# Two attention blocks on one core: the remainder of P by DMA in 30 steps at other places, wq in quarter loads, the first x in three parts, output written in place

## The chip, the cores and the metric

The kernel runs on one core of one Trainium2 chip. The metric is the device time of one execution in microseconds (us). Profiles show one execution; the engines are called PE (TensorE matmul), PEld (its weight loads), DVE (VectorE), ACT (ScalarE), POOL (GpSimd) and SP (SyncE, which here only issues DMAs).

## The reference, cut to what matters

Two independent problems A and B of the same shapes, each a query projection, attention of grouped queries over a cache, and an output projection; the outputs are joined on the last axis. All inputs are bf16.

```python
B, Sq, D = 16, 80, 576
Hq, Hkv, Sk, Dh = 32, 16, 512, 128
def _A_ref(x, k_cache, v_cache, wq, wo):
    rep = Hq // Hkv                       # 2 query heads share one K/V head
    q = transpose((x @ wq).reshape(B, Sq, Hq, Dh), 0, 2, 1, 3)
    k = jnp.repeat(k_cache, rep, axis=1)  # k_cache, v_cache: (B, Hkv, Sk, Dh)
    v = jnp.repeat(v_cache, rep, axis=1)
    scores = jnp.einsum("bhqd,bhkd->bhqk", q, k) * (Dh ** -0.5)
    p = softmax(scores, axis=-1)
    o = jnp.einsum("bhqk,bhkd->bhqd", p, v)
    return transpose(o, 0, 2, 1, 3).reshape(B, Sq, Hq * Dh) @ wo
# B is the same with its own inputs
return jnp.concatenate([a, b], axis=-1)
```

## The kernel before

The work is cut into 128 **units**. A unit is one batch row and four K/V heads, so eight query heads of 80 rows: 640 rows of scores against 512 keys. These are five blocks of 128 rows: block 0 is the **remainder** (the last 32 of the 160 rows of each of the four K/V heads, put together), blocks 1 to 4 are the first 128 rows of each head.

For each unit, in this order:

- SP loads K with a transposing DMA (L631, one for two units) into one of three pairs of slots, and V (L635) into one of six slots.
- PE makes the scores: the remainders of two units together (L665, `SR`, in tiles of 32 columns), the other blocks in one matmul each (L678, `S`).
- DVE takes the negated maximum (L687), ACT the exponential with the row sum (L691), DVE the reciprocal (L697), POOL multiplies P by it (L700; `poolr` is the stream of the remainder, `pool` that of the other blocks). Remainders of P have four slots, the other blocks twelve.
- PE transposes P in pieces of 64 by 128 (L733, `T`): 40 matmuls, of which eight are the remainder's. ACT or DVE copies the result to `pT` (L751, L752; the remainder's part L757, L758, twice per unit).
- In some units, `rtr`, the remainder is transposed by a DMA from SBUF to SBUF instead (L740, stream `RT`, issued by SP): then `T` has 32 matmuls and the two copies of the remainder fall away. Before, these are the 27 odd units from 71 to 123. The DMA waits for POOL's normalisation of the remainder; PV of the unit waits for the DMA, and so does the exp that next writes the slot of P that it reads.
- PE multiplies `pT` by V (L781, `PV`), and ACT or DVE copies the result to `oT` (L795).

The query projection of an octet of query heads (L542, `Q`, four matmuls of 128 rows of D and the last 64 rows by L555, which stands in `T` or, at the start, in `QT`) is spread over earlier units; ACT or DVE copies it, scaled, to `qT` (L568, L569). Its weights are loaded eight times (four times for each problem) into one of two slots: `ldwa` at L507 and two small `ldwt` at L511. Before, the first two of these loads come in four pieces of 256 columns, the other six in one piece of 1024 KB.

The first problem's x is loaded (L380) and transposed on PE (L401, L419; POOL copies the last 64 columns beside them, L388); eight matmuls on zeros and ones (L353, `warm`) go ahead of that. The identity that the transposes need is made by POOL (L340). x lies, as bf16, in the memory of `acc`, the float32 accumulator of the output.

The output projection (L827, `P`, eight matmuls of 288 columns per half step) is also spread; the first half of the heads is copied to `acc` (L839), the second half is added to it by DVE into one of two slots of `osb` (L856), and SP stores the slot (L862): 40 stores.

Nothing is scheduled while the kernel runs. Each operation is put into a stream, sorted there by a key, and a string of 5227 operations (`ORDER`) gives the order over all streams: a letter names the stream, an apostrophe the second choice of engine (ACT in place of DVE for the copies), digits the PSUM banks. Each engine runs its operations in this order, and SP's queue is one of these: a DMA that waits holds all that stand behind it. Semaphore waits follow from reads and writes (`finalize`).

The names of the change in the old code:

```python
rtr = RT0 <= U < RT1 and (RTM[U % 2] or U >= RT2)          # L717
S.add("sp", 5.0 * U - 0.4, em_rtr, reads=[R(("P", psls[0]), ("n", 5 * U))],
      writes=[R(("pR", pts, h), U) for h in range(2)], dsem="d_r%d" % pts, ...)
pieces = () if half else [(256 * i_, 256 * i_ + 256) for i_ in range(4)] if goct < W4 else ((0, 1024),)
```

Of the kernel before, what the change touches and what calls it, by code (L numbers as in the profile page):

```python
# [26 lines left out]
NOSB = 2  # L27
NWARM = 8
# [3 lines left out]
RT0 = 71  # L32
RT1 = 124
RTM = (0, 1)
RT2 = 999
LQ = 12
# [15 lines left out]
XLD = ((-100.0, -85.0), (-5.0, -4.9))  # L52
# [3 lines left out]
W4 = 2  # L56
# [214 lines left out]
def bass_concat_heads__gqa_block_cached__gqa_block_cached__near_ridge_kernel(  # L271
# [27 lines left out]
    with ExitStack() as es:  # L299
# [33 lines left out]
        def R(res, ver):  # L333
            return (res, ver)
# [606 lines left out]
```

## Time and profile before

| what | value |
|---|---|
| time, median of 3 runs (lowest, highest) | 720.46 us (718.11, 721.86) |
| the profiled execution, its own time | 720.92 us |
| its span, first to last instruction | 719.0 us |
| granted TensorE clock | 1.00 |
| PE / PEld busy | 712.0 / 508.8 us |
| DVE / ACT / POOL busy | 630.0 / 637.5 / 431.9 us |
| a transposing load of K for two units, issue to landing | 8.4 to 8.5 us |
| a load of V | 5.0 to 5.2 us |
| a remainder of P by DMA | 4.2 us |
| wq: 256 KB / 1024 KB at a time | 4.7 / 6.9 to 8.4 us |
| a store of the output | 3.8 us |

Busy is the time that an engine's records cover. Matmuls are pipelined, so a covered PE need not be at its peak; the starts of matmuls say more. A line such as `SPq L740` is an entry of SP's queue. In the timeline the columns are start, duration, engine, line, operation, tiles and count; brackets give the idle time before and what ended it. In the windows the columns are the window, its length, then for each engine its busy time and number of instructions.

### The profile page before, as it was taken

The page shows a single profiled execution, that of the slowest core. Times are in us where ns is not written, and L with a number is a line of the kernel's source. Part 1 is how long each engine was busy: PE and PEld are TensorE (multiplying, and loading weights), DVE is VectorE, ACT ScalarE, POOL GpSimd, SP SyncE. Part 2 cuts the span into 40 slices and gives each one's busy share as a digit, 9 for nine tenths or more (in the row PEclk, how much of TensorE's full clock was granted, in tenths as well). Part 3 has the DMA queues.
Part 4 walks back from the last instruction along what each step waited for, and adds up shares of the span by engine and source line. Part 5 has one row for each costly group of instructions (what it writes and reads, how often), then busy time and mean ns, then how long its engine had stood idle before and what let it go on. Part 6 is the DMA issues. An engine that isn't in the chain of part 4 may idle for free.

```text
span 719.0 us, 25863 instructions
## 1 busy us (share of the span) xinstructions
PE 712.0 (99%) x10604; PEld 508.8 (71%) x10604; DVE 630.0 (88%) x1419; ACT 637.5 (89%) x1830; POOL 431.9 (60%) x650
## 2 busy tenths in 40 slices
PE   9999999999999999999999999999999999999998
PEld 5576777777777777777777776767677777777777
DVE  3999998899978998899998899878898889998995
ACT  1999998899988998799988999888999898998994
POOL 0467657566655765755774566645676466665783
PEclk9999999999999999999999999999999999999999
DMA  9999999999799998999999999999999999999970
GB/s 238 275 217 240 273 252 250 286 232 244 175 268 241 220 241 194 258 223 240 255 216 248 226 201 206 228 246 239 220 229 204 279 196 261 225 247 221 211 195 18
DMA packets 388853, 164.23 MB, mean 228 GB/s; under 512 B 293248, under 2 KB 385664, under 8 KB 388736
## 3 DMA queue, kind: packets, MB, share of 16 engines
q1 hardware_dynamic: 388736, 162.59, 100.2%
q8 instruction: 84, 1.38, 0.8%
q14 instruction: 33, 0.27, 0.2%
HBM read 87.65 MB, written 2.95 MB: 126 GB/s over the span
## 4 chain that ended last, share of the span: by engine, by line
PE 93%; DMA 2%; DVE 2%; ACT 1%; SPq 0%; issue 0%; ACTq 0%; DVEq 0%
PE ps L827 22%; PE ps L781 20%; PE ps L542 18%; PE ps L678 15%; PE ps L733 10%; PE ps L665 5%; PE ps L555 4%; DVE negmax L687 2%; DMA pT<-p_sb 1%; DMA wq_sb<-in_A_wq_dram 1%; DMA out_dram<-osb 1%; ACT p_sb L691 0%; ACT qT L568 0%; DVE xT L406 0%; DVE qT L569 0%
## 5 line engine op out<-in xcount | busy, mean ns | idle before, releaser
L700 POOL TENSOR_SCALAR p_sb<-p_sb,rinv 128x512 bf16<-128x512 bf16 x640 | 430.1, 692 | 271.4 <-DVE rinv L697 270.8
L691 ACT ACTIVATE p_sb<-ps,negmax 128x512 bf16<-128x512 f32 x640 | 442.7, 713 | 27.3 <-DVE negmax L687 23.5
L687 DVE TENSOR_REDUCE negmax<-ps 128x1 f32<-128x512 f32 x640 | 419.2, 682 | 35.0 <-PE ps L678 30.3
L781 PE MATMUL ps<-pT,v_sb 128*128 128x160 bf16 x2048 | 191.2, 233 | 1.1 <-ACT p_sb L691 0.8
L781 PEld LDWEIGHTS ps<-pT,v_sb 128*128 128x128 bf16 x2048 | 152.8, 98 | 42.6 <-ACT p_sb L691 4.1
L827 PE MATMUL ps<-wo_sb,oT 128*128 128x288 bf16 x1280 | 181.1, 286 | 0.0
L678 PE MATMUL ps<-kT,qT 128*128 128x512 bf16 x512 | 178.0, 380 | 1.2 <-ACT p_sb L691 0.8
L542 PE MATMUL ps<-xT,wq_sb 128*128 128x320 bf16 x1024 | 174.4, 299 | 0.2 <-DMA wq_sb<-in_A_wq_dram 0.2
L827 PEld LDWEIGHTS ps<-wo_sb,oT 128*128 128x128 bf16 x1280 | 122.0, 98 | 42.5 <-ACT p_sb L691 0.8
L691 ACT ACTIVATION_READ_ACCUMULATOR p_sb<-ps,negmax 128x1 f32 x640 | 146.0, 228 | 0.0
L542 PEld LDWEIGHTS ps<-xT,wq_sb 128*128 128x128 bf16 x1024 | 95.4, 98 | 45.0 <-ACT p_sb L691 2.4
L751 ACT COPY pT<-ps 128x512 f32<-128x512 f32 x157 | 92.4, 602 | 13.3 <-PE ps L733 12.8
L733 PEld LDWEIGHTS ps<-ident,p_sb 64*128 64x128 bf16 x4904 | 88.2, 95 | 7.3 <-issue 1.3
L733 PE MATMUL ps<-ident,p_sb 64*128 64x64 bf16 x4904 | 92.4, 190 | 0.3 <-issue 0.2
L752 DVE COPY pT<-ps 128x1024 bf16<-128x1024 bf16 x99 | 67.3, 684 | 11.4 <-PE ps L733 10.0
L568 ACT ACTIVATE qT<-ps 128x320 bf16<-128x320 f32 x133 | 59.0, 458 | 19.3 <-PE ps L555 15.5
L569 DVE TENSOR_SCALAR qT<-ps 128x320 bf16<-128x320 f32 x123 | 58.2, 482 | 10.7 <-PE ps L555 6.1
L795 DVE CAST oT<-ps 128x320 bf16<-128x320 f32 x122 | 58.4, 482 | 7.7 <-PE ps L781 7.4
L678 PEld LDWEIGHTS ps<-kT,qT 128*128 128x128 bf16 x512 | 48.0, 97 | 24.1 <-ACT p_sb L691 4.1
L795 ACT CAST oT<-ps 128x320 bf16<-128x320 f32 x134 | 58.9, 451 | 5.2 <-PE ps L781 4.9
L697 DVE RECIPROCAL rinv<-rowsum 128x3 f32<-128x3 f32 (+1 forms) x256 | 38.4, 160 | 1.8 <-ACT p_sb L691 1.7
L665 PE MATMUL ps<-kT,qT 128*32 128x512 bf16 x512 | 39.2, 384 | 0.0
(31 smaller groups left out, 175.5 us busy)
## 6 DMA issues: line engine op xcount, KB each, us to landing
v_sb<-in_A_v_cache_dram SPq DMA_DIRECT2D x64, 512.0 KB, 5.0
v_sb<-in_B_v_cache_dram SPq DMA_DIRECT2D x64, 512.0 KB, 5.2
wo_sb<-in_A_wo_dram SPq DMA_DIRECT2D x8, 576.0 KB, 5.8
wo_sb<-in_B_wo_dram SPq DMA_DIRECT2D x8, 576.0 KB, 5.8
wq_sb<-in_B_wq_dram SPq DMA_DIRECT2D x4, 1024.0 KB, 6.9
out_dram<-osb SPq DMA_DIRECT2D x40, 72.0 KB, 3.8
wq_sb<-in_A_wq_dram SPq DMA_DIRECT2D x8, 256.0 KB, 4.7
wq_sb<-in_A_wq_dram SPq DMA_DIRECT2D x2, 1024.0 KB, 8.4
```

Source lines behind the costliest of these rows:

```text
L542: last = e.matmul(ps[:, vbq[h].phys, QO:QO + 320], lhsT=wq_sb[:, wsl, ck, hi * 128:(hi + 1) * 128], rhs=xT[:, half, ck, n0:n0 + 320], star ...
L665: last = e.matmul(ps[32 * g4:32 * g4 + 32, vb_.phys, :], lhsT=qT[:, qsl_, bl_, g4 * 160 + 128:g4 * 160 + 160], rhs=k_of(U_, g4), start=Tru ...
L678: return e.matmul(ps[:, vb.phys, :], lhsT=qT[:, qsl, bl, gl * 160:gl * 160 + 128], rhs=k_of(U, gl), start=True, stop=True)
L687: return e.tensor_reduce(negmax[:, si:si + 1], ps[:, vb.phys, :], axis=AX.X, op=AluOpType.max, negate=True)
L691: return e.activation(p_sb[:, psl, :], ps[:, vb.phys, :], AF.Exp, bias=negmax[:, si:si + 1], scale=1.0, accum_out=rowsum[:, ss, k:k + 1])
L700: return e.tensor_scalar(p_sb[:, psl, :], p_sb[:, psl, :], rinv[:, ss, k:k + 1], 1.0, op0=AluOpType.mult, op1=AluOpType.mult)
L733: last = e.matmul(dst, lhsT=p_sb[64 * h:64 * h + 64, psls[k_], j * 128:(j + 1) * 128], rhs=ident[64 * h:64 * h + 64, 64 * h:64 * h + 64], ...
L751: return e.copy(dst.bitcast(F32), ps[:, vtp[h].phys, :].rearrange("p (j n) -> p j n", j=4))
L752: return e.tensor_copy(dst, psb[:, vtp[h].phys, :].rearrange("p (j n) -> p j n", j=4))
L781: last = e.matmul(ps[:, vo.phys, off:off + 160], lhsT=v_sb[:, vs, gl, j * 128:(j + 1) * 128], rhs=pT[:, pts, j, :, 32 * gl:32 * gl + 32], ...
L795: return (e.copy if en == "act" else e.tensor_copy)(dst, src)
L827: last = e.matmul(ps[:, vb.phys, 0:DC], lhsT=oT[:, sp_ * (HH // 2) + i, rb * 128:(rb + 1) * 128], rhs=wo_sb[:, 2 * c3 + sp_, i, :], start= ...
```

## The change

- `RTS` replaces `RT0`, `RT1`, `RTM` and `RT2`: the remainder goes by DMA in the odd units of 9 to 23, 41 to 47, 73 to 79 and 97 to 123, 30 in all.
- `W4 = 99`: all eight loads of wq come in four pieces of 256 columns, each with its own semaphore.
- The first half of x is loaded in three parts (one, two and two blocks of 128 rows); the first part is issued by ACT, the others by SP. POOL's copies of x are ordered after the identity.
- Six warm matmuls in place of eight.
- The second half of the output is added in place: DVE writes bf16 into the memory of `acc`, and the store reads it there; `osb` is gone, and each of the 20 places has its own semaphore.
- `ORDER` is a new string of 5246 operations (30 for 27 remainder steps, 18 more issues of wq, and what goes with the third part of x).

```diff
-NOSB = 2
-NWARM = 8
+NWARM = 6
-RT0 = 71
-RT1 = 124
-RTM = (0, 1)
-RT2 = 999
+RTS = ((9, 24), (41, 48), (73, 80), (97, 124))
-XLD = ((-100.0, -85.0), (-5.0, -4.9))
+XLD = ((-100.0, -99.9, -85.0), (-5.0, -4.9))
+XENG = (("act", "sp", "sp"), ("sp", "sp"))
-W4 = 2
+W4 = 99
...
-        XP = ((0, 3), (3, 5))
+        XPS = (((0, 1), (1, 3), (3, 5)), ((0, 3), (3, 5)))
...
-                S.add("sp", XLD[half][part], em_ldx,
+                S.add(XENG[half][part], XLD[half][part], em_ldx,
...
-                S.add("pool", xk, em_xrp, reads=[R(("xs", half * NRT + k_), 0) for k_ in range(k0, k1)],
+                S.add("pool", xk, em_xrp, reads=[R(("xs", half * NRT + k_), 0) for k_ in range(k0, k1)] + [IDENT],
...
-            rtr = RT0 <= U < RT1 and (RTM[U % 2] or U >= RT2)
+            rtr = U % 2 == 1 and any(a_ <= U < b_ for a_, b_ in RTS)
...
-                                return e.tensor_tensor(osb[:, slot, :], ps[:, vb.phys, 0:DC],
+                                return e.tensor_tensor(xs[:, rb, 2 * c3 * DC:(2 * c3 + 1) * DC], ps[:, vb.phys, 0:DC],
                                                        acc[:, rb, c3 * DC:(c3 + 1) * DC], AluOpType.add)
...
-                                return e.dma_start(dst, osb[:, slot, :])
+                                return e.dma_start(dst, xs[:, rb, 2 * c3 * DC:(2 * c3 + 1) * DC])
...
-                                  writes=[R(("osb", slot), (prob, half, n))], name="oeb%d.%d.%d" % (prob, half, n),
+                                  writes=[R(("acc", rb, c3), (prob, hh))], name="oeb%d.%d.%d" % (prob, half, n),
...
-                                  dsem="d_out%d" % slot, name="st%d.%d.%d" % (prob, half, n), stream="st")
+                                  dsem="d_out%d" % (2 * rb + c3), name="st%d.%d.%d" % (prob, half, n), stream="st")
```

More of the change, by code (lines that the diff above doesn't have):

```diff
@@ L376, in bass_concat_heads__gqa_block_cached__gqa_block_cached__near_ridge_kernel @@
             x_ap = probs[0][0]
[L377 removed]
+            for part, (k0, k1) in enumerate(XPS[half]):
                 def em_ldx(e, x_ap=x_ap, half=half, k0=k0, k1=k1):
@@ L887, in run_engine @@
             if name == "sp":
-                for i in range(NOSB):
+                for i in range(2 * NPP * NRT):
                     n = "d_out%d" % i
```

153 lines of the change are left out of this document (75 added, 78 removed).

## The prediction

> **What bounds the kernel now.** I read the busy time by windows of 20 us first, since a share over the whole span would hide where TensorE rests.
>
> ```profile
> core 0: us, PE busy (x) PEld busy (x) DVE busy (x) ACT busy (x) POOL busy (x), PEclk, DMA share, GB/s
> 0.00:20.00 20.00, 18.16 (x124) 10.62 (x125) 6.82 (x19) 3.81 (x8) 1.32 (x8) 1.00 1.03 243
> 20.00:40.00 20.00, 19.48 (x266) 11.45 (x265) 20.00 (x47) 19.89 (x60) 12.05 (x20) 1.00 1.14 241
> ...
> 80.00:100.00 20.00, 20.00 (x324) 14.60 (x319) 19.08 (x44) 19.19 (x57) 13.93 (x21) 1.00 1.12 283
> ...
> 480.00:500.00 20.00, 19.19 (x296) 14.00 (x293) 15.64 (x33) 16.64 (x48) 11.34 (x17) 1.00 1.09 227
> 500.00:520.00 20.00, 19.54 (x270) 13.39 (x268) 17.47 (x39) 18.85 (x55) 12.47 (x19) 1.00 1.11 232
> ...
> 700.00:719.00 19.00, 16.40 (x263) 13.23 (x260) 10.25 (x24) 8.23 (x26) 6.71 (x10) 1.00 0.07 22
> sum 719.00, PE 712.01 PEld 508.80 DVE 629.99 ACT 637.53 POOL 431.91; mean PE 19.78 PEld 14.13 DVE 17.50 ACT 17.71 POOL 12.00
> ```
>
> TensorE (PE) rests for 719.0 - 712.0 = 7.0 us: 1.84 in the first window, 0.52 in the second, nothing from 40 to 400, 2.02 in six windows between 400 and 700 (0.16, 0.24, 0.81, 0.46, 0.26, 0.09), and 2.60 at the end. That could be an illusion of long matmul records, so I took the starts of matmuls in the trace one after the other: inside a group they stand 0.122 (L827), 0.069 (L781) and 0.136 us (L542) apart nearly everywhere, always the same, and all excesses over these add up to 8.9 us, of which 3.6 before 20 us, 1.4 from 20 to 40 and 3.3 after 400. So PE truly streams, some 706 us of work, and a change can win only from the rests.
>
> The rests after 400 us I followed into the timeline and the waits:
>
> ```profile
> 482.53 0.51 SPq L635 DMA_DIRECT2D v_sb<-in_B_v_cache_dram  x1
> ...
> 483.85 0.44 PE L781 MATMUL ps<-pT,v_sb 128*128 128x160 bf16 x4 [0.81 <-ACT p_sb L691]
> ```
> ```profile
> 516.38 0.69 ACT L691 ACTIVATE p_sb<-ps,negmax 128x512 bf16<-128x512 f32 x1 [0.64 <-DMA pT<-p_sb]
> ```
> ```profile
> pT<-p_sb SPq DMA_TRANSPOSE x27, 4.2
> ```
>
> The first is the PV of unit 83, named as freed by ACT; but that unit's remainder transpose (rtr, 27 of them, L740) was issued at 478.9 and landed at 483.8, just when PE went on. The second is an exp that wants a p_sb slot which the transpose of unit 89 still reads (issued 510.6, landed 516.3). Units 71 and 109 rest likewise (landings 417.6 and 624.8, 0.3 and 0.1 us before the PV). So nearly all of the 3.3 us belongs to late remainder transposes, most of it near the load of wq (482.0).
>
> The queue that issues everything, SP, I read last:
>
> ```profile
> 78.34 1.86 SPq L635 DMA_DIRECT2D v_sb<-in_A_v_cache_dram  x1
> 80.25 6.67 SPq L631 DMA_TRANSPOSE kT<-in_A_k_cache_dram  x1
> 86.96 1.13 SPq L635 DMA_DIRECT2D v_sb<-in_A_v_cache_dram  x2
> 88.14 6.73 SPq L631 DMA_TRANSPOSE kT<-in_A_k_cache_dram  x1
> 94.91 1.13 SPq L635 DMA_DIRECT2D v_sb<-in_A_v_cache_dram  x2
> 96.09 6.58 SPq L631 DMA_TRANSPOSE kT<-in_A_k_cache_dram  x1
> ```
>
> From 20 to 103 us SP never pauses: a pair of units costs it 8.9 us (one K transpose, two V), and PE eats a pair in 9.9 (first scores of units 6 and 16 at 44.4 and 93.9). Supply is barely ahead there: K lands 0.6 us before its first use for units 6 and 7, 1.0 for 12, 3.3 for 16, 6.7 for 18; V 0.1 us for unit 7, 3.5 for 12, 3.8 for 13. Later, margins are 5 to 15 us.
>
> **The change part by part,** against the profiled execution: 720.92 us around a span of 719.0, 0.46 above the median of 720.46.
>
> Fewer transposes on PE. Three more units leave the remainder to DMA, 30 for 27. A unit then has 32 transposes in place of 40; the trace starts one pair every 0.029 us, so 4 pairs save 0.115, three units 0.35 us, and two copies of 0.28 us each on DVE or ACT. In return the new order string changes between full tiles and the 64- or 32-row tiles 339 times instead of 335 (I counted both strings), and each costs 0.096 us (a score matmul is followed after 0.216 us by a full tile, after 0.311 by a 64-row one): +0.38. Together 0.0.
>
> Where the 30 stand. Units 71 and 81 to 95 go back to PE; units 9 to 23 and 41 to 47 are new. The rests of 71, of 83 (with 0.24 just before it) and of 89 go away: 0.16 + 0.24 + 0.81 + 0.46 = 1.67 us of rest, 2.5 by the starts of matmuls, where pauses that record ends cover count too. The 12 new ones may rest anew. I measured in both strings the PE work between an rtr and its unit's PV: in before the rests come where it is 3.6 to 4.7 us (a landing takes 4.2, at most 5.7), and not in all such places. The new string has eight places at or under 5.1 us, as before has, three of them new (units 21, 45, 47: 4.6, 4.9, 4.5). So I price the new ones at the mean of before, 3.3 us / 27 = 0.12 each, 1.4 together. Net -1.1; ends -3.3 (all rests gone) and +1.0 (the three late by the longest landing).
>
> SP's queue in the early stretch. An rtr waits in SP for the Pool's normalisation, and behind it wait K and V. RT0 (unit 9) comes when its data is ready (68.8 us; SP arrives at 69.1) and costs 1.2 us of issue. RT1 (unit 11) stands after V11, which ended at 80.2, now 81.4; its normalisation ended at 82.7. So SP stands 1.3 us, issues until 83.9, and the K of units 16 and 17 starts 3.7 us later than 80.25, with a margin of 3.3. Then V12 at 91 instead of 87.0 (+4.2, margin 3.5); RT2 (unit 13) finds six normalisations moved ahead of it (87.0 + 6 x 0.69 = 91.2); V13 goes at 92.4 (+4.8, margin 3.8, and its PV stands 1.2 us of PE work later in the new string); the next K at 93.6 (+5.5, margin 6.7); the one after it at 101.5 (+5.4, margin 6.2). PE is late by 0.2 to 1.0 us by this sum, less what the pause of SP lets the full DMA engines (share 1.12) drain. Bounds: 0 below, and above 4, where a late score delays the next normalisation and so the next rtr. I take +0.5, nearer to the sum.
>
> wq in four pieces. Six 1024 KB loads become 24 of 256 KB, 18 more issues of 0.5 us on SP. No PE wait on wq shows after 20 us (only 0.2 at the start), so the earlier first piece wins nothing. The issues are hidden by SP's waits for free K slots (144.6 us on the score matmuls alone); without this cover three issues hold the K or V behind them by 1.5 us a load. Taken 0; ends -0.3 and +1.
>
> First x in three, six warm matmuls. The chain to the first scores ends elsewhere:
>
> ```profile
> 10.01 5.71 SPq L631 DMA_TRANSPOSE kT<-in_A_k_cache_dram  x1
> ...
> 19.45 0.38 PE L678 MATMUL ps<-kT,qT 128*128 128x512 bf16 x1 [0.36 <-ACT qT L568]
> ```
>
> This K landed at 19.3 and is issued after the same 14 loads in both strings; ACT's copy came at 19.4. PE had 0.5 us to spare there, and two warm matmuls (0.43 each) add 0.9 more. All that x gains is waited off again: -0.1, with ends -0.5 and +0.4. The Trainium skill (DMA: Bandwidth & Descriptors, Issuing engines are not separate DMA queues) says that issuing from another engine saves only the sequencer's time; the issue of x takes 0.45 us here, so by it alone this part could be worth at most that, and the sum stays.
>
> Output in place. No wait of the output add on a store stands among the waits; it waits for PE (6.1 us, 9 times). The end stays: the last add at 716.44 (0.46 us), then the store. 0; should the stores have held the add unseen, a slot would come free after 3.8 us.
>
> Sum: 0.0 - 1.1 + 0.5 - 0.1 = -0.7, so 720.2 on this execution and 719.7 on the median.
>
> **Rivals.** *All rests go and none come.* -3.3 after 400, -1.0 of the 1.4 between 20 and 40 through another order, and -0.3: 716 us. For it: the worst places near the wq load are gone; against it: as many short distances as before.
>
> *SP held behind the early rtr.* This ends on the other side. If K of units 16 to 21 lands as slowly after its issue as now (10.3 us), each lateness moves the normalisation that the next rtr waits for, and RT1 to RT5 each add 1 us: +4 to +6, so 725 on the median. It decides where that K is issued after 83.5 us (80.2 plus the margin). For it: SP without pause and ACT and DVE at 19 to 20 of 20; against it: SP's pauses empty the DMA queues, and margins grow by themselves after unit 18.
>
> *A cold TensorE.* The 512-column warm matmuls start every 0.43 us, the later ones every 0.22; the change comes at about 6.1 us. With six, PE may rest before x lands, and the fast rate come one stretch later: 16 matmuls of L542 at twice 0.136 lose 2.2 us, less the 1.4 spare: +0.8, 720.5 on the median. The Trainium skill (TensorE: Matmul & The Clock Gate, What's actually happening) puts the rise after a busy window of some 3.4 us; the trace shows 4.9 us from the first matmul, and no run here with fewer.
>
> *No effect in sum.* Wins and losses cancel: 720.5.
>
> **How the numbers follow.** Forecast 0.44 (718 to 722); all rests gone 0.20; SP held 0.22; cold 0.06; nothing 0.08. A measurement of this kernel tells about 0.5%, 3.6 us, from no change: faster is under 716.9, slower above 724.1. Faster: most of the second case and a little of the first, 0.20. Slower: nearly all of the third, 0.21. Same: 0.59. The range reaches to 715.8, which holds the gain case, and to 725.5, which holds the middle of the SP case.
>
> **What would show it.** PE's rest in 480 to 520 us falls from 1.27 to under 0.4; new rests of 0.2 to 0.8 us stand at units 21, 45 or 47; the third K after RT1 lands with a margin under 2 us; first scores still start at 19.3 to 19.5; the tail after the last matmul stays 2.6. A rest of over 1 us on a score matmul between 85 and 115 us would prove the SP case; less than 1.5 us of rest between 20 and 700 in all, the gain case.

## The result, and the profile after

The changed kernel is slower: 725.12 us in the median (722.23 to 726.61) against 719.18 us (717.80 to 721.86) for the kernel before, run beside it; the ratio is 1.0071, 95% interval 1.0055 to 1.0087. The prediction was 719.7 us and "the same". The profiled execution of after took 726.61 us around a span of 724.9, that of before 720.92 around 719.0. That execution of after is the slowest of nine and one of three with a mean TensorE clock under 1 (725.20 to 726.61 us; the other six have a median of 723.9), so what its profile shows of a slowed clock is no part of those six. Lines of the changed kernel have other numbers: scores L674, PV L777, P (output product) L822, Q L538, the wt product L551, exp L687, normalisation L696, copies of P to pT L747 and L748, K L627, V L631, remainder transpose (rtr) L736, wq L503, wt L507, output add L851. In the kernels of the experiments all of these are shifted by one or by a few lines.

The same view by windows, after:

```profile
core 0: us, PE busy (x) PEld busy (x) DVE busy (x) ACT busy (x) POOL busy (x), PEclk, DMA share, GB/s
0.00:20.00 20.00, 17.39 (x124) 9.71 (x124) 7.69 (x21) 3.87 (x8) 1.50 (x9) 1.00 1.08 250
20.00:40.00 20.00, 19.39 (x268) 11.59 (x268) 19.89 (x47) 20.00 (x60) 12.63 (x20) 1.00 1.15 240
...
60.00:80.00 20.00, 19.54 (x278) 13.79 (x277) 18.91 (x43) 18.87 (x55) 11.61 (x18) 1.00 0.88 214
...
120.00:140.00 20.00, 16.96 (x250) 12.04 (x250) 12.99 (x31) 15.79 (x43) 12.10 (x18) 1.00 1.15 232
140.00:160.00 20.00, 20.00 (x302) 14.55 (x294) 16.78 (x37) 16.31 (x46) 11.06 (x17) 0.91 1.02 254
160.00:180.00 20.00, 19.20 (x309) 13.41 (x307) 17.30 (x40) 18.64 (x57) 13.48 (x21) 1.00 1.15 242
480.00:500.00 20.00, 20.00 (x314) 14.65 (x306) 16.59 (x34) 18.19 (x55) 10.20 (x16) 1.00 0.93 234
500.00:520.00 20.00, 20.00 (x290) 14.22 (x290) 18.24 (x43) 19.02 (x57) 13.40 (x21) 1.00 1.00 229
600.00:620.00 20.00, 19.04 (x289) 12.84 (x288) 17.99 (x42) 17.59 (x51) 13.05 (x21) 1.00 1.10 221
640.00:660.00 20.00, 18.68 (x265) 13.16 (x263) 16.34 (x39) 16.15 (x45) 12.22 (x19) 1.00 0.98 198
```

Two of these windows before the change:

```profile
120.00:140.00 20.00, 20.00 (x288) 14.64 (x287) 16.90 (x40) 16.75 (x48) 10.59 (x16) 1.00 0.99 265
140.00:160.00 20.00, 20.00 (x317) 14.57 (x316) 18.73 (x45) 18.69 (x54) 13.17 (x21) 1.00 0.96 247
```

TensorE's total is 712.1 us, as before (712.0), though some 1.6 us of after's are a slower clock. So the work is nearly the same, and the 5.9 us are rest and that clock. The rests of 480 to 520 us are gone, as predicted, but others stand at 600 to 660, and a new hole stands at 120 to 140 us, where before had 20.00 of 20. In 140 to 160 us PE is busy throughout, but the granted clock (PEclk) is 0.91. The starts of matmuls, with every excess over the spacing inside a group added up, give the balance by stretch:

| us of excess | before | after |
|---|---|---|
| 0 to 40 | 4.9 | 4.8 |
| 40 to 115 | 0.2 | 1.2 |
| 115 to 170 | 0.0 | 5.8 |
| 170 to 400 | 0.2 | 0.2 |
| 400 to the end | 3.5 | 3.2 |
| all | 8.9 | 15.2 |

The count takes in matmuls at a slower clock, which stand further apart. So +6.3 us by this count, against +5.9 of span, and the stretch from 40 to 170 us alone has +6.8. The waits of PE name the releasers (total us, times, longest):

```profile
PE ps L551 <- DMA wt<-in_A_wq_dram: 2.1, 1, 2.1
PE ps L777 <- ACT p_sb L687: 1.6, 2, 1.3
...
PE ps L777 <- ACT pT L747: 0.9, 1, 0.9
PE ps L661 <- DMA kT<-in_A_k_cache_dram: 0.8, 1, 0.8
```

All four are late DMAs. The wt of the fifth head group, 2.1 us, is the largest; the 0.9 at 127.2 us is a PV (unit 17) whose rtr was issued at 120.7 and landed at 127.1; the 0.8 is the K of unit 28; the longer of the two "p_sb" waits is the PV of unit 113, whose rtr was issued at 645.3 and landed at 651.5. (The view names the engine whose semaphore came last; the landings say that it was the transfer.) What makes the first three late is on SP's queue (start, us of issue):

```profile
64.62 0.58 SPq L631 DMA_DIRECT2D v_sb<-in_A_v_cache_dram  x1
70.21 1.19 SPq L736 DMA_TRANSPOSE pT<-p_sb  x1
71.44 1.13 SPq L631 DMA_DIRECT2D v_sb<-in_A_v_cache_dram  x2
72.62 6.13 SPq L627 DMA_TRANSPOSE kT<-in_A_k_cache_dram  x1
...
83.98 5.18 SPq L627 DMA_TRANSPOSE kT<-in_A_k_cache_dram  x1
89.20 0.58 SPq L631 DMA_DIRECT2D v_sb<-in_A_v_cache_dram  x1
92.60 1.19 SPq L736 DMA_TRANSPOSE pT<-p_sb  x1
...
111.40 8.57 SPq L627 DMA_TRANSPOSE kT<-in_A_k_cache_dram  x1
120.02 0.58 SPq L631 DMA_DIRECT2D v_sb<-in_A_v_cache_dram  x1
120.70 1.19 SPq L736 DMA_TRANSPOSE pT<-p_sb  x1
121.93 0.59 SPq L503 DMA_DIRECT2D wq_sb<-in_A_wq_dram  x1
...
130.06 1.19 SPq L736 DMA_TRANSPOSE pT<-p_sb  x1
131.30 2.21 SPq L503 DMA_DIRECT2D wq_sb<-in_A_wq_dram  x3
133.54 2.41 SPq L507 DMA_DIRECT2D wt<-in_A_wq_dram  x2
...
156.15 12.12 SPq L627 DMA_TRANSPOSE kT<-in_A_k_cache_dram  x2
```

Before the rtr of unit 9 SP is done at 65.20 and stands until 70.21, 5.0 us, for the normalisation, which ends at 70.18. Before that of unit 13 it stands from 89.78 to 92.60, 2.8 us, and here the normalisation had ended at 89.10: the step waits for something else. `pT` has two slots, so the rtr of a unit writes the slot that PV of the unit two before still reads, and PV of unit 11 ends at 92.57:

```profile
91.29 1.28 PE L777 MATMUL ps<-pT,v_sb 128*128 128x160 bf16 x16
```

The waits of SP for all rtr of after name PE more often than the normalisation:

```profile
SPq L736 <- PE ps L674: 22.9, 11, 3.7
...
SPq L736 <- POOL p_sb L696: 11.9, 8, 2.8
```

With its other lines PE comes to 42.1 us there. In before it is 40.5 us on PE and 9.8 on the normalisation. The description of the kernel and the prediction name only the normalisation. Of the eight early steps, those of units 13, 21 and 23 stand for a PV (2.8, 1.8 and 0.3 us), that of unit 9 alone for the normalisation, and the other four do not stand. While SP stands before unit 9, nothing new reaches the DMA engines, and they run dry:

```profile
67.00:68.00 1.00, 1.00 (x14) 0.77 (x12) 1.00 (x4) 1.00 (x5) 0.00 (x0) 1.00 1.01 345
68.00:69.00 1.00, 1.00 (x47) 0.82 (x44) 1.00 (x3) 1.00 (x5) 0.84 (x2) 1.00 0.10 35
69.00:70.00 1.00, 1.00 (x15) 0.71 (x8) 1.00 (x4) 1.00 (x4) 1.00 (x2) 1.00 0.06 16
70.00:71.00 1.00, 1.00 (x9) 0.65 (x7) 0.92 (x3) 0.98 (x4) 1.00 (x3) 1.00 0.00 0
```

From there on SP is late for 90 us. Set beside the issues of the same loads in before, K of units 16, 18 and 20 goes 3.7, 6.9 and 7.4 us later, K of 22, 24 and 26 4.7, 6.4 and 6.5, and that of unit 28 10.1 us later (156.15 against 146.03; 3.9 us of this is PE, which by then is late itself). The wt of the fifth group goes at 133.54 instead of 111.55: it stands behind the last quarter of wq and two more rtr. The lines of before for these two:

```profile
111.55 0.63 SPq L511 DMA_DIRECT2D wt<-in_A_wq_dram  x1
...
146.03 11.45 SPq L631 DMA_TRANSPOSE kT<-in_A_k_cache_dram  x2
```

### The profile page after: what moved, and what is told of

Same layout as the page of the kernel before. It is cut to its first block, busy times and chain, and to the rows that moved or that the text cites. A ratio compares the mean times of both kernels' runs of the same rounds, so it can differ in the third digit from the quotient of the medians.

```text
span 724.9 us, 25853 instructions
## 1 busy us (share of the span) xinstructions
PE 712.1 (98%) x10578; PEld 508.1 (70%) x10578; DVE 629.3 (87%) x1420; ACT 637.8 (88%) x1824; POOL 432.5 (60%) x651
## 4 chain that ended last, share of the span: by engine, by line
PE 91%; DMA 4%; ACT 3%; SPq 1%; issue 0%; DVE 0%; ACTq 0%
PE ps L822 20%; PE ps L777 19%; PE ps L538 18%; PE ps L674 15%; PE ps L729 10%; PE ps L661 5%; PE ps L551 4%; ACT p_sb L687 2%; DMA kT<-in_A_k_cache_dram 2%; DMA wt<-in_A_wq_dram 1%; DMA pT<-p_sb 1%; DMA acc<-in_A_x_dram 1%; ACT qT L564 1%; ACT pT L747 0%; SPq L503 0%
## 5 line engine op out<-in xcount | busy, mean ns | idle before, releaser
L696 POOL TENSOR_SCALAR p_sb<-p_sb,rinv 128x512 bf16<-128x512 bf16 x640 | 430.5, 692 | 276.8 <-DVE rinv L693 275.9
L687 ACT ACTIVATE p_sb<-ps,negmax 128x512 bf16<-128x512 f32 x640 | 443.3, 710 | 34.2 <-DVE negmax L683 24.1
L777 PE MATMUL ps<-pT,v_sb 128*128 128x160 bf16 x2048 | 188.8, 234 | 3.0 <-ACT p_sb L687 1.6
L777 PEld LDWEIGHTS ps<-pT,v_sb 128*128 128x128 bf16 x2048 | 153.1, 98 | 41.3 <-ACT p_sb L687 5.1
L822 PE MATMUL ps<-wo_sb,oT 128*128 128x288 bf16 x1280 | 181.6, 286 | 0.0
L674 PE MATMUL ps<-kT,qT 128*128 128x512 bf16 x512 | 178.0, 381 | 1.4 <-ACT p_sb L687 1.2
L538 PE MATMUL ps<-xT,wq_sb 128*128 128x320 bf16 x1024 | 175.1, 300 | 0.0
L822 PEld LDWEIGHTS ps<-wo_sb,oT 128*128 128x128 bf16 x1280 | 121.9, 98 | 42.2 <-issue 0.8
L687 ACT ACTIVATION_READ_ACCUMULATOR p_sb<-ps,negmax 128x1 f32 x640 | 144.2, 225 | 0.0
L538 PEld LDWEIGHTS ps<-xT,wq_sb 128*128 128x128 bf16 x1024 | 95.2, 98 | 45.8 <-ACT p_sb L687 2.0
L747 ACT COPY pT<-ps 128x512 f32<-128x512 f32 x156 | 90.9, 598 | 15.0 <-PE ps L729 14.3
L564 ACT ACTIVATE qT<-ps 128x320 bf16<-128x320 f32 x139 | 62.0, 459 | 17.0 <-PE ps L551 14.9
L748 DVE COPY pT<-ps 128x1024 bf16<-128x1024 bf16 x100 | 68.0, 683 | 8.4 <-PE ps L729 7.4
L791 DVE CAST oT<-ps 128x320 bf16<-128x320 f32 x129 | 61.6, 482 | 9.8 <-PE ps L777 8.9
L674 PEld LDWEIGHTS ps<-kT,qT 128*128 128x128 bf16 x512 | 48.4, 97 | 27.4 <-ACT p_sb L687 6.0
L565 DVE TENSOR_SCALAR qT<-ps 128x320 bf16<-128x320 f32 x117 | 55.8, 482 | 9.7 <-PE ps L551 6.9
L791 ACT CAST oT<-ps 128x320 bf16<-128x320 f32 x127 | 55.4, 446 | 7.1 <-PE ps L777 6.6
L551 PE MATMUL ps<-xT,wt 64*128 64x320 bf16 x256 | 39.0, 306 | 2.2 <-DMA wt<-in_A_wq_dram 2.1
```

Source lines behind the costliest of these rows:

```text
L538: last = e.matmul(ps[:, vbq[h].phys, QO:QO + 320], lhsT=wq_sb[:, wsl, ck, hi * 128:(hi + 1) * 128], rhs=xT[:, half, ck, n0:n0 + 320], star ...
L564: return e.activation(dst, src, AF.Identity, scale=SCALE)
L674: return e.matmul(ps[:, vb.phys, :], lhsT=qT[:, qsl, bl, gl * 160:gl * 160 + 128], rhs=k_of(U, gl), start=True, stop=True)
L687: return e.activation(p_sb[:, psl, :], ps[:, vb.phys, :], AF.Exp, bias=negmax[:, si:si + 1], scale=1.0, accum_out=rowsum[:, ss, k:k + 1])
L696: return e.tensor_scalar(p_sb[:, psl, :], p_sb[:, psl, :], rinv[:, ss, k:k + 1], 1.0, op0=AluOpType.mult, op1=AluOpType.mult)
L747: return e.copy(dst.bitcast(F32), ps[:, vtp[h].phys, :].rearrange("p (j n) -> p j n", j=4))
```

## Experiments

Each ratio is against the kernel before, run in the same session on the same chip, with its 95% interval. The kernel before had medians from 719.2 to 720.7 us in these sessions, so ratios are to be compared and not times. Each kernel has an `ORDER` of its own, changed no further than its edit asks for; the cuts below show the other lines. "Rest" is the excess of the table above, from one profiled execution of each kernel. The questions were: which part loses the time, what about that part, and whether anything of the new string is worth keeping.

**The parts alone.** Three kernels have one part of the change in the kernel before, and one has the early rtr there.

Quarters of wq, wt behind them:

```diff
-W4 = 2
+W4 = 99
```

> The kernel before, in which only the six later loads of wq come in quarters, issued one behind the other, with wt behind them as in the changed kernel. Theory 'order of wt': a rest of 1 to 2 us where unit 20 wants wt, ratio 1.002 to 1.004. Theory 'early remainder steps': SP has time here, no rest, ratio 0.999 to 1.001; 18 more issues of 0.5 us are hidden.

Measured 720.06 us, 1.0007 (0.9989 to 1.0025), no rest over 0.2 us between 40 and 170. The quarters alone cost nothing that can be told.

The output added in place (the store reads acc, osb is gone):

```diff
-e.tensor_tensor(osb[:, slot, :], ...
+e.tensor_tensor(xs[:, rb, 2 * c3 * DC:(2 * c3 + 1) * DC], ...
```

> The kernel before, in which only the output of the second half is added in place and stored from there (the order string is the same). Theory 'hidden' (the stores were never waited for, the end is the last add and its store): no change, ratio 0.998 to 1.002. Rival 'the stores from acc are slower or the 20 semaphores at the end cost': ratio 1.002 to 1.004, with a tail after the last matmul over 3.5 us (2.9 before).

Measured 718.87 us, 0.9998 (0.9987 to 1.0009).

The start (x in three parts, the first issued by ACT, six warm matmuls, the first operations in the order of after):

```diff
-NWARM = 8
-XLD = ((-100.0, -85.0), (-5.0, -4.9))
+NWARM = 6
+XLD = ((-100.0, -99.9, -85.0), (-5.0, -4.9))
```

> The kernel before, in which only the start is that of the changed kernel: x in three parts, the first issued by ACT, six warm matmuls, and the order of the first 92 operations. Theory 'covered by K': first scores at 19 to 19.8 us as before, ratio 0.998 to 1.002. Rival 'cold start': with six warm matmuls and a pause of PE the slow matmuls last into the first projections in some executions, first scores up to 1.5 us later, ratio 1.001 to 1.003.

Measured 719.91 us, 1.0010 (0.9998 to 1.0023). None of these three can be told from the kernel before; their medians together make 0.0015 of the 0.0071.

Units 9 to 23 by rtr in the string of before, 35 in all:

```diff
-rtr = RT0 <= U < RT1 and ...
+rtr = (9 <= U < 24 and U % 2) or RT0 <= U < RT1 and ...
```

> The kernel before, in which only the eight odd units from 9 to 23 have their remainder transposed by DMA too (35 steps), with the steps at places in SP's order like those of the changed kernel. Theory 'early remainder steps': rests of 3 to 6 us between 60 and 180 us, less 0.9 us of PE work, ratio 1.003 to 1.007. Theory 'order of wt': wt and wq are issued early here, so no long rest, ratio 0.998 to 1.001.

Measured 741.19 us, 1.0299 (1.0277 to 1.0320): four times the loss of after. My places for them were bad ones, and the profile shows how such a step loses:

```profile
81.58 6.52 SPq L630 DMA_TRANSPOSE kT<-in_A_k_cache_dram  x1
88.14 1.27 SPq L739 DMA_TRANSPOSE pT<-p_sb  x1
```

The rtr of unit 11 stands behind a K load whose issue takes 6.5 us, so it goes at 88.1; PE rests 6.7 us from 86.7 on, and as much again at 161.8, where unit 23 stands behind K of 28. So I moved five K loads behind the rtr they stood ahead of:

> The kernel before with the eight early remainder steps (units 9 to 23) once more, now each ahead of the K load that it stood behind in e4 (K of units 16, 18, 20, 26 and 28 waits behind it). Theory 'an early step is late when it stands behind a K load, or makes K late when ahead of it': the rests of 6.6 us at 87 and 162 us go, rests of 0.5 to 2 us stay, 3 to 6 us in all between 60 and 180 us; ratio 1.003 to 1.008. Theory 'string' (the loss of the changed kernel lies in other places of its order): no rest over 0.3 us in 60 to 180, ratio 0.998 to 1.000.

Measured 740.57 us, 1.0298 (1.0265 to 1.0332). A miss: the rests only moved (7.1 us at 160, 3.8 at 122). In this kernel two rtr hold SP for 11 us:

```profile
137.11 11.01 SPq L739 DMA_TRANSPOSE pT<-p_sb  x2
```

The 11 us are SP standing between the two, 8.6 us before the rtr of unit 21 for PV of unit 19; before that of unit 19 it had stood 6.6 us for PV of unit 17. Neither of the two placements tried is a free place in the old string: ahead of K the step waits and holds K, behind K it comes late for its own PV.

**Undoing in the changed kernel.** First the largest wait by itself: the wt of the two groups gets a stream of its own and goes ahead of the quarters.

```diff
-... name="ldwt%d.%d" % (goct, r), stream=strm if goct < W4 else "wt")
+... name="ldwt%d.%d" % (goct, r), stream=strm if goct < 2 else "wt")
```

> The changed kernel, in which only the two small loads of wq's last 64 rows (wt) of octets 4 and 5 go ahead of the first quarter instead of behind the fourth. Theory 'order of wt' (the quarter loads put wt at the end of their stream, and that is what PE waits for at 137 us): the 2.2 us wait goes, and with it the slow matmuls right after it, so 3 us faster than the changed kernel (about 722, ratio to before 1.003). Theory 'early remainder steps' (SP is late as a whole in units 17 to 29, wt is only the first to be seen): the wait moves to the first quarter of wq or to K of unit 28, and no more than 1 us is won (ratio 1.006 to 1.008).

Measured 725.18 us, 1.0064 (1.0040 to 1.0089). The wait for wt is gone and the time is the same: PE now rests 1.5 us before 100.9 for the V of unit 13 and 1.5 before 157.2 for the rtr of unit 23. So the wt was where SP's lateness came out, not its source.

All eight early rtr back on TensorE:

```diff
-RTS = ((9, 24), (41, 48), (73, 80), (97, 124))
+RTS = ((41, 48), (73, 80), (97, 124))
```

> The changed kernel, in which only the eight odd units from 9 to 23 have their remainder transposed on PE again (22 steps by DMA). Theory 'early remainder steps': the rests of PE between 40 and 170 us (7.0 us in the changed kernel) fall under 1 us; PE has 8 x 0.115 = 0.9 us more to do; 5 us faster, ratio to before 1.000. Theory 'order of wt': wt still stands behind the four quarters, so half of the loss or more stays, ratio 1.004 or above.

Measured 722.95 us, 1.0049 (1.0030 to 1.0068). Rest between 40 and 170 us falls from 7.0 to 1.1 us. SP does not stand, and its K goes 6.4, 6.7 and 8.0 us earlier than in after:

```profile
64.54 1.68 SPq L630 DMA_DIRECT2D v_sb<-in_A_v_cache_dram  x3
66.27 7.64 SPq L626 DMA_TRANSPOSE kT<-in_A_k_cache_dram  x1
...
77.24 8.04 SPq L626 DMA_TRANSPOSE kT<-in_A_k_cache_dram  x1
...
87.05 7.80 SPq L626 DMA_TRANSPOSE kT<-in_A_k_cache_dram  x1
```

But only about a third of the loss came back (1.0071 to 1.0049, intervals that overlap). This kernel pays TensorE work for eight more units (0.9 us) and their copies, and has 1.9 us of rest between 170 and 400 us where after has 0.2. That these two are the difference is argued from the profile, not isolated.

**The halves.** The order of before up to the scores of unit 57 (some 330 us), then that of after, and the reverse:

> The order of before up to the scores of unit 57 (about 330 us), then the order of after: its remainder steps (units 73 to 79 and 97 to 123), its wq load in quarters for the last two octets, its output in place. Theory (the loss comes from SP running late behind the early remainder steps, so it lies in the first half): no rest over 0.3 us between 40 and 170 us, ratio to before 0.997 to 1.002. Rival (the new string is slower all along, by tile changes and fewer remainder steps): 1.003 to 1.005.

> The order of after up to the scores of unit 57, with its early remainder steps (units 9 to 23 and 41 to 47), quarters of wq for four octets, x in three parts and output in place, then the order of before with its steps in units 71 to 123. Theory: it carries the whole loss of after, 1.006 to 1.010, with 5 to 8 us of rest between 40 and 170 us. Rival (the second half of the new string carries a good part): 1.002 to 1.005.

Measured 720.74 us, 1.0018 (1.0004 to 1.0031) for the old half first, and 723.15 us, 1.0049 (1.0019 to 1.0080) for the new half first. The first is as the theory had it; the second fell into the range of the rival. The two add up to 1.0067, near after's 1.0071, so by the medians the first half carries some seven tenths of the loss. The old half first has no rest over 0.1 us between 40 and 170; the new half first has 4.2 us there, the largest at the same PV as after (1.1 at 98.7) and for wt (1.3 at 137.5).

**How many steps, or which.** Units 17 to 23 back on TensorE, 9 to 15 kept:

```diff
-RTS = ((9, 24), ...
+RTS = ((9, 16), ...
```

> After with the remainder of units 17, 19, 21 and 23 back on TensorE; the steps of units 9 to 15 stay by DMA. Theory (SP falls behind by some 1 us with each early step and is caught up by about 1 us a pair when there is none): SP is late at V13 and the K of units 16 to 19, a rest of about 0.5 us stands at 98, but the large rests at 126, 137 and 166 us go, under 2 us in all between 40 and 170; ratio 1.004 to 1.006. Rival (the first steps alone set the lateness, as the prediction's SP case had it): over 4 us of rest between 40 and 170 us, ratio 1.007 or more.

Measured 724.54 us, 1.0063 (1.0034 to 1.0092), between the two readings; the rest is the rival's, over 4 us, with one of 2.4 us from 98.6 on for the V of unit 13 and a stretch of slow matmuls behind it. The first steps alone make SP late enough. Then the two steps before which SP stood longest: unit 9 back, and units 9 and 13 back.

```diff
-RTS = ((9, 24), ...
+RTS = ((11, 24), ...
```

> After with the remainder of unit 9 alone back on TensorE; the seven steps of units 11 to 23 stay by DMA. Theory (SP stood 5.0 us before the step of unit 9, 65.2 to 70.2 in the profile of after, and that set K and V of units 12 on late by 6 us for good): the K that went at 72.6 goes near 66.5, rests between 40 and 170 us fall from 7.0 to under 3.5, ratio 1.003 to 1.006. Rival (each of the eight steps costs about the same): 6 us of rest, ratio 1.0065 or more.

> After with the remainder of units 9 and 13 back on TensorE, the two before which SP stood longest (5.0 and 2.8 us). Theory of the standing: under 2 us of rest between 40 and 170 us, as with all eight given back (1.1 there), ratio 1.004 to 1.0055. Rival (each step costs about the same): 5 us of rest, ratio 1.006 or more.

Measured 721.63 us, 1.0025 (1.0004 to 1.0046) and 721.88 us, 1.0023 (1.0005 to 1.0042). One step of thirty given back takes the ratio from 1.0071 to 1.0025, and these two intervals do not overlap. By the median it is more than giving back all eight (1.0049), but there they do. Both ratios are below what either reading said. In the kernel with unit 9 back:

```profile
66.57 1.68 SPq L630 DMA_DIRECT2D v_sb<-in_A_v_cache_dram  x3
68.29 8.38 SPq L626 DMA_TRANSPOSE kT<-in_A_k_cache_dram  x1
```

No stand here, and K at 68.3 in place of 72.6. But SP now stands 4.1 us before the rtr of unit 13 (87.74 to 91.83, again for PV of unit 11), and K of unit 18 goes as late as in after:

```profile
91.83 1.19 SPq L735 DMA_TRANSPOSE pT<-p_sb  x1
...
95.32 7.30 SPq L626 DMA_TRANSPOSE kT<-in_A_k_cache_dram  x1
```

What is won shows later: K of units 26 and 28 go 3.4 and 2.8 us earlier than in after. Rest between 40 and 170 us is 3.3 us (one of 2.1 from 104 on, for the K of unit 18), with unit 13 back as well 2.1.

Unit 9 alone kept, the other seven back:

```diff
-RTS = ((9, 24), ...
+RTS = ((9, 10), ...
```

> After with the remainder of units 11 to 23 back on TensorE and unit 9 alone by DMA, the step before which SP stood 5.0 us. Theory of the standing: the K after it goes near 72.5, 6 us late, V of unit 13 or the K of units 14 to 18 rests PE by 0.5 to 2 us between 75 and 110, then the lateness is made up where SP waits for free slots (from 105 us on); ratio 1.005 to 1.006. Rival (one step is caught up by the margins): rests as with all eight given back, 1.1 us, ratio 1.0045 to 1.005.

Measured 723.35 us, 1.0042 (1.0025 to 1.0058). SP stands 3.7 us (65.8 to 69.5), K goes at 72.2, 83.5 and 92.7 (in after at 72.6, 84.0 and 95.0), and yet the rest between 40 and 170 us is 1.2 us: the rival was right. One stand is absorbed by the margins and made up by 110 us, where K goes at 109.9 against 109.3 with none of the eight. It costs where further steps follow and use up the room to catch up. That profile also shows a step that after's profile let pass: the rtr of unit 45, one of the tight places of the prediction (issued at 267.8), lets PE rest 2.7 us for the PV, and an exp waits for the same transpose:

```profile
274.46 0.69 ACT L686 ACTIVATE p_sb<-ps,negmax 128x512 bf16<-128x512 f32 x1 [0.58 <-DMA pT<-p_sb]
...
274.52 1.76 PE L776 MATMUL ps<-pT,v_sb 128*128 128x160 bf16 x12 [2.73 <-ACT p_sb L686]
```

**SP's queue or the DMA engines.** V of units 14 to 31 issued by GpSimd:

```diff
-S.add("sp", 5.0 * U - VK, em_ldv,
+S.add("pool" if 14 <= U < 32 else "sp", 5.0 * U - VK, em_ldv,
```

> After with the V loads of units 14 to 31 issued by GpSimd's queue in place of SP's; all eight early steps stay. It takes 0.6 us an issue from SP and lets V pass a step that SP stands before; K stays behind the steps. Theory (V and K are late because SP holds them): no wait of a PV on V or of an exp behind it, K 1 us a pair earlier, rests between 40 and 170 us fall to 3 to 5 us, ratio 1.004 to 1.007. Rival (the DMA engines themselves are full, whoever issues): rests as in after, 6 to 8 us, ratio 1.007 or more; or GpSimd's issues hold the normalisations and it gets slower still, 1.01.

Measured 743.42 us, 1.0285 (1.0245 to 1.0326), the last of the readings named, and nearly three times what I gave it. PE waits on V:

```profile
PE ps L776 <- DMA v_sb<-in_A_v_cache_dram: 11.1, 5, 4.0
PE ps L660 <- DMA kT<-in_A_k_cache_dram: 2.4, 1, 2.4
```

V lands 8.1 us after its issue by GpSimd (median; 5.3 from SP). Two things make it late. V of unit 15 stands behind a normalisation, for which GpSimd waits 8.5 us, and is issued at 109.97. V of units 16 and 17 are issued at 115 and land 16.2 and 18.6 us later. The run separates these no further, so whether the DMA engines are full, whoever issues, stays open.

**The middle and late steps.** Units 41 to 47 back as well as 9 to 23:

> After with the remainder of units 9 to 23 and also of units 41 to 47 back on TensorE, 18 steps left. It measures the four middle steps against the kernel that gave back only 9 to 23 (1.0049). Theory: those four cost nothing that stands out, so this one is 0.5 us of TensorE work slower, 1.005 to 1.007. Rival (the 1.7 us of rest between 170 and 400 us there come from the middle steps): 1.002 to 1.004, with under 0.5 us of rest there.

Measured 723.77 us, 1.0059 (1.0041 to 1.0078), against 1.0049 with those four kept; its 2.4 us of rest between 170 and 400 us are waits of PE on copies of DVE and ACT (qT, p_sb, pT), which get two more copies with each unit that is given back. So the middle steps are no cost in the mean.

In the kernel before, the late rests that the prediction read: units 71, 83 and 109 back on TensorE, and the K of unit 94 behind the rtr of 89.

> The kernel before, in which only units 71, 83 and 109 go back to PE (24 steps by DMA), and K of unit 94 stands behind the step of unit 89 instead of ahead. By the prediction's step that these late steps cost PE 0.48, 0.97, 0.43 and 0.76 us by the starts of matmuls: 2.6 us less rest, 0.35 us more work, so 2.2 us faster, ratio 0.997. Rival 'the rests only move to the next late step': ratio 0.999 to 1.001.

Measured 723.07 us, 1.0055 (1.0038 to 1.0072). A miss for the prediction's reading: rests after 400 us are 4.9 us instead of 3.5, at other places (524, 546, 624). So the late rests do not go away with these steps. The edit also moves a K load, and no run separates the two.

**What is left.** After with units 9, 13, 21, 23, 45 and 47 back, 24 steps by DMA, and the same with the later wq loads whole again:

> After with the remainder of units 9, 13, 21, 23, 45 and 47 back on TensorE, 24 steps left: the two before which SP stood, the two beside the wq quarters, and the two tight ones of the middle, one of which rested PE by 2.9 us in the profile of the kernel with unit 9 alone. Theory (the loss is the standing of SP and single tight steps; PE work as in before): rests between 40 and 400 us under 1.5 us, ratio 0.999 to 1.002. Rival (the new string costs its 2 us whatever the steps, by evictions and quarters): 1.003 to 1.005.

> The same, and the six later wq loads whole again (one of 1024 KB at the place of the last quarter, 18 issues of 0.5 us fewer). Theory (quarters are worth at most 0.5 us here): within 0.001 of the kernel with quarters. Rival (the quarters cost what the kernel alone could not show, 1.0007 with an interval to 1.0025): 0.002 lower.

Measured 721.86 us, 1.0014 (0.9996 to 1.0032) and 723.04 us, 1.0028 (1.0011 to 1.0045). The first can't be told from the kernel before, though its rest between 40 and 400 us is some 2 us where under 1.5 was expected; whole wq loads make it no better. No version was faster than the kernel before; of those that keep early steps this one is nearest to it.

## Why the prediction was wrong

**The step that failed** is "SP's queue in the early stretch": +0.5 was taken between 0 and "above 4", and this stretch cost 6.8 us of rest and clock in the profile. The lateness itself was walked nearly right: K of units 16, 18 and 20 later by 3.7, 5.5 and 5.4 was forecast, and 3.7, 6.9 and 7.4 came. Four things were wrong in it. First, the walk let SP arrive at the rtr of unit 9 at 69.1 and find its data ready at 68.8. That arrival was a time of before, where K of 12 took 7.60 us to issue with two V ahead of it; in the new string one V stands ahead, K takes 5.85, SP arrives at 65.2, and the normalisation ends at 70.2. A stand of 0 became one of 5.0. That the K of unit 16 was 3.7 us late all the same is luck: the walk had SP stand 1.3 us before the rtr of unit 11, and there it does not stand (it arrives at 82.2, the normalisation ended at 81.9). Second, the wait for the slot of `pT` was left out. The walk gave the rtr of unit 13 its data at 91.2; the normalisation ended at 89.1, and the step went at 92.6, behind PV of unit 11. Third, the walk ended at K of 20, with "margins grow by themselves after unit 18". They grow only while SP can run ahead; the rtr of units 17 to 23, two wq loads in quarters and the wt behind them came next, and SP was still 6.5 us late at K of 26 and 10.1 at K of 28. All large early rests (126.0, 137.2, 166.1) lie behind the end of the walk. Fourth, the lateness was turned into time by its overshoot over the margin of one load; but a late SP meets one small margin after the other: V of 13, the rtr of 17, wt, K of 28.

**The rival "SP held behind the early rtr"** had the queue and the time (725) at a chance of 0.22. Its mechanism did not show: it let each lateness delay the next normalisation and so the next rtr, but after unit 9 no early rtr waited for a normalisation. Its condition (K of 16 issued after 83.5) was met by 0.5 us, 83.98. Its place was not met: the rests come from 98 us on and mostly after 125, on PV, wt and K, not on score matmuls between 85 and 115. That the first steps alone bring a loss of this size is shown by the kernel that keeps 9 to 15 (1.0063; half of its executions have the slowed clock of the last section, and the other half has a median of 721.5 us), that the step of unit 9 is needed for the whole of it by the one that gives back unit 9 alone (1.0025, though there SP stands before unit 13 instead), and that it needs followers by the one that keeps unit 9 alone (1.2 us of rest).

**Fewer transposes on PE, 0.0**: right within what can be told. The starts of matmuls have 6.3 us more of excess in 5.9 us more of span, so the work fell by 0.4; the equal busy times (712.1 and 712.0) don't show it alone, since the slower clock stands in the first.

**Where the 30 stand, -1.1**: the rests at 71, 83 and 89 went, as said, and 480 to 520 us rests 0 in place of 1.27. But 107 and 113 rest instead (1.0 and 1.5 us), so after 400 us only 0.3 us are won. The price per step from one profile was the fault: rests after 400 us in kernels with the same steps there were 3.5, 4.1, 2.4 and 1.1 us (before, and before with in-place output, quarters, and the new start). Of the tight units 21, 45 and 47 none rested in after's profile, and unit 45 by 2.7 us in another kernel's: a tight place is a chance of a rest, not a price.

**wq in four pieces, 0**: right for the quarters alone (1.0007) and with them undone at the end (no gain). What it overlooked is that wt moves behind the last quarter, from 111.6 to 133.5, and PE waited 2.1 us for it; taking that wait away won nothing, since SP was late in any case.

**First x and six warm, -0.1; output in place, 0**: right within what can be told (1.0010 and 0.9998). First scores start at 19.05 (19.3 to 19.5 was said), and the tail stays 2.6 us. The cold case did not come about in this profile. It did in that of the kernel with wt ahead, which has the same start: matmuls of the first projections stand 0.267 us apart until 10.4 us (0.136 in after from 6.7 us on), and the first scores start at 20.65, 1.7 us after their K landed.

**What stays open**: without any early step the ratio is still 1.0049, and its parts are argued only. The old half first is 1.0018 although its rests are fewer than in before, which has nine more late steps by DMA; part of it is TensorE work (nine units of 0.115 us), the rest was not followed. And whether a longer DMA queue for K alone would end the lateness was not tried.

## What to carry to other kernels

A DMA that waits is priced by where the issuing queue stands when it gets there, in the new order, and by all that it waits for: the data that it reads and the slot that it writes. The time that the queue then stands is taken from everything behind it, whether the step itself is in time or not. Walk the queue on until its lateness is gone, past the end of the change if need be, and meet every small margin on the way, not only that of the next load. And where a rest stands in one profile only, ask a second one before counting it as won.

## What was unexpected of the hardware

A rest of some 2 us on PE can cost nearly as much again. In after PE waits 2.13 us, and soon after it runs at half clock (windows of 2 us; column after POOL is the granted clock):

```profile
139.65 0.31 PE L551 MATMUL ps<-xT,wt 64*128 64x320 bf16 x2 [2.13 <-DMA wt<-in_A_wq_dram]
```

```profile
140.00:142.00 2.00, 2.00 (x49) 0.98 (x41) 1.41 (x4) 1.38 (x5) 0.00 (x0) 0.68 1.00 206
142.00:144.00 2.00, 2.00 (x13) 1.57 (x12) 0.90 (x4) 1.77 (x5) 1.75 (x3) 0.50 1.26 290
```

That is 0.32 x 2 + 0.50 x 2 = 1.6 us lost on top of the 2.1. It happened also after rests of 2.20 us (units 9 to 15 kept) and 2.73 us (unit 9 alone, clock 0.60 and 0.54), and not after one of 2.07 us (unit 9 back). The Trainium skill (TensorE: Matmul & The Clock Gate, What's actually happening) has the slow clock come back after an idle window of about 3.4 us; here shorter rests were enough, so the measurement decides. What decides between 2.07 and 2.13 us is where the rest lies. By the clock records of the traces each slow stretch after the start lasts 3.41 us or two or three times that, and changes come on a grid of 3.41 us. In the kernels just named the rest left 2.13 us (137.31 to 140.73), 2.08 (99.04 to 102.46) and 2.62 (271.00 to 274.42) of one step of this grid idle, and the slow clock began at its end; the rest of 2.07 us fell into two steps, 1.45 and 0.62. In all profiles of these runs that have such records the slow clock follows a step with 2.08 us or more of rest (eleven times), and none with 1.51 or less. The slow clock may also be why executions of these kernels spread more: with units 9 to 15 kept the runs lie between 719.4 and 730.6 us, and the six runs above 726 are the ones with a mean clock under 1; the other six are all under 722.5.

The issue of a DMA transpose on SP is no fixed cost. The K of unit 22 took 8.57 us to issue in after, where SP had not stood since the rtr of unit 13, and 3.88 us in the kernel without early rtr, where SP had just waited for a slot:

```profile
109.32 3.88 SPq L626 DMA_TRANSPOSE kT<-in_A_k_cache_dram  x1
```

I read this as waiting for room in the DMA queue, which no run isolates. The Trainium skill (DMA: Bandwidth & Descriptors, Issuing engines are not separate DMA queues) calls the sequencer's time for starting a DMA usually small beside the DMA; for the 32 K loads of the first problem in after the issue is 3.9 to 8.7 us, 6.0 in the median, where the median from the start of the issue to the landing is 9.3. So the measurement decides here too: for these loads the issue is most of it.
